# First stage of an MLP on seven half products, one more batch transposed through HBM, and a new plan of steps

## Chip, core and metric

The kernel runs on one core of a Trainium2 chip. The time is the device time of one execution in microseconds (us). Engines: PE (TensorE, matmuls; PEld is its weight load), DVE (VectorE), ACT (ScalarE), POOL (GpSimd, which also issues the loads' DMAs) and SP (whose queue issues stores and the DMAs of the round trips through HBM).

## What is computed

```python
# q, k, v: (8 batches, 8 heads, 576 rows, 64), float32
k_p = k.reshape(B, H, 72, 8, D).mean(axis=3)            # keys and values pooled by 8
v_p = v.reshape(B, H, 72, 8, D).mean(axis=3)
attn = softmax(q @ k_p.T / sqrt(D));  x = attn @ v_p     # x as (8, 576, 512)
h = relu(x.T @ w_tok1) @ w_tok2;      u = x + h.T        # w_tok1 (576, 256), w_tok2 (256, 576)
out = u + relu(u @ w_ch1) @ w_ch2                        # w_ch1 (512, 1536), w_ch2 (1536, 512)
```

## The kernel before

**Units.** The channel MLP (last line above) is done in nine units of 512 rows: unit n takes 512 of the 576 rows of batch n, and unit 8 takes the 64 rows left over of each of the eight batches. Everything else (pooling, scores, softmax, token MLP) is cut into named steps of batch n+1, n+2 and so on, and these are put between the matmuls of unit n.

**One unit.** First stage: 12 tiles of 128 hidden columns (`l1_tile`, L517), each 4 matmuls with 512 columns of `uT` (u transposed, 128 channels on partitions) as the moving side and a 128x128 block of `w_ch1` as weights, into one of four PSUM banks p1a to p1d; ACT writes relu of it to `GT` (L521). Second stage: the product with `w_ch2` in seven half-size products in place of eight (a Strassen-Winograd scheme), each 12 matmuls of 256 columns (`product`, L583). In order: x and y (both on plain `GT`), z, x again, w, z again, x again; unit 8 leaves w out and does its last two on x. DVE makes the sums of `GT` that they need: steps `=3`, `=1`, `=2`, `=4` (L545, L557), on 128x1536, into `area`; sums of `w_ch2` are made once (`w0` to `w3`). DVE also evacuates every product (L626), adding the residual u and earlier products. All of that is in program order on each engine.

**The plan.** `PLAN[n]` says which steps are recorded after which chunk of unit n. A chunk is what PE does between two yields: two matmuls of 512 columns in the first stage, four of 256 in the second. A normal unit has 45 chunks (24, then 3 for each of seven products). The plan fixes the order on each engine, and nothing else; each engine goes as fast as its waits allow. Steps named here: `b.K0 b.K1 b.V0 b.V1` pool k and v of batch b on POOL (L174 to L180); `b.kpT` transposes the pooled keys on PE (L222); `b.s0` to `s2` scores and exp; `b.av0` to `av4` the product with v; `b.at0 b.at1` and `b.u0` to `u4` the token MLP; `b.lk b.lq b.lv` loads. `g` is a gate: DVE sets a flag and POOL copies it (L712, L713), so that what POOL has next, a load or a pooling, starts no sooner than DVE gets there; the next gate's flag waits for the copy. `HEAD` is the same kind of list for what comes before unit 0; `d3` in it is three filler matmuls on zeros.

**From u to uT.** Two ways. Batches 1 and 2: steps `t0` to `t3`, each four 128x128 PE transposes into PSUM (L424) and one ACT copy (L425). Batches 3 to 7 (`BOUNCED`) and the left-over rows: u is spilled to HBM (`M0`, `M2`, for the left-over rows `M4`), read back by four DMAs (`M`, `MT`), all on SP's queue, and each of `T0` to `T3` (`T4`, `T5`) transposes it in 32x32 blocks on DVE (L458). The rows of u then lie in another order ("paired"), and an evacuation with such a residual is two DVE instructions of 256 columns in place of one of 512. Batch 0 has a way of its own through matmuls.

**Buffers.** Four PSUM banks are handed out by `take` and `give`, two more pairs are a pool of two (`ps_two`). `raw` holds two buffers each of loaded k, v and q.

The functions that the diff touches, as they were:

Of the kernel before, what the change touches and what calls it, by code (L numbers as in the profile page):

```python
# [8 lines left out]
FP32 = mybir.dt.float32  # L9
BF16 = mybir.dt.bfloat16  # L10
# [7 lines left out]
SYNC = mybir.EngineType.SP  # L18


HEAD = """LkA LkT LkB LvT Lq LvA LvB Lt1 Lk1 Lt2 Lc1b Lc1a Lq1 Lc1c Lv1 Lc1d p1 Lc2a Lc2b Lc2c d2 d2 d3 d1 d4 d4 c0 c1 prep q0 kp0 kp1 kt0 q1 d1 o0 kt1 kp2 e0 e1 q3 kt2 o1 q2 e3 vpool0 o3 e2 a00 vpool1 a02 o2 m01 d1 d1 m00 a04 X1 m03 a14 m02 X0 m04 p0 a10 a12 1.kpool m10 m14 m12 m13 m11 A1 A0 X2 X3 A2 A3"""
PLAN = [
# [9 lines left out]
]  # L32


# [1 line left out]
def kernel(  # L36
# [15 lines left out]
    B, H, S, D = q.shape  # L52
    P = 128
    POOL = 8
    BOUNCED = range(3, B)
    SP = S // POOL
    BP, BR = 64, S // 64
    NE = (BR + 1) // 2
# [60 lines left out]
                            in_=src[b, h0:h1].rearrange("h (j i) d -> j h (i d)", i=POOL)[j0:j1])  # L119

    def load_kv(b, src, key):
        t = loaded[b, key] = raw.tile([SP, H, POOL, D], BF16, name=key + "r")
        kv(t, src, b, 0, H, 0, BP)
        kv(t, src, b, 0, H, BP, SP)

# [3 lines left out]

    def first_kv(key, part):  # L130
        if (0, key) not in loaded:
            loaded[0, key] = raw.tile([SP, H, POOL, D], BF16, name=key + "r")
# [381 lines left out]
    def l1_tile(n, m, uT):  # L514
        ps = take([P, 512], FP32)
        for kk in range(4):
            nc.tensor.matmul(out=ps, lhsT=w_ch1[:, kk, m * P:(m + 1) * P], rhs=uT[kk],  # L517
                             start=(kk == 0), stop=(kk == 3))
            if kk == 1:
                yield  # L520
        nc.scalar.activation(out=GT[:, m, :], in_=ps, func=AF.Relu)  # L521
        give(ps)
        yield
# [39 lines left out]
    def weight_sum(k):  # L563
# [7 lines left out]
        else:  # L571
            sub(T[:, 3], w_ch2[:, sec, lo], T[:, 1])

    def unit_fast(n, u):
        last = n == B
        uT = [u["uT"][:, kk, :] for kk in range(4)]
        for m in range(NM):
            yield from l1_tile(n, m, uT)

        def product(ps, a, w, start, after, split=False, end=None):  # L580
            for i in range(2):
                for m in range(NH):
                    nc.tensor.matmul(out=ps[i] if split else ps[:, i], lhsT=chunk(u, i, a(m)), rhs=w(m),  # L583
                                     start=start and m == 0 and (i == 0 or split), stop=(m == NH - 1),
                                     skip_group_check=True)
                    if (i * NH + m) % 4 == 3 and (i, m) != (1, NH - 1):
                        yield
                if split:
                    after(i)
            if not split:  # L590
                after(slice(0, 2))
            if end is not None:
                give(end)
            yield

        def bank(split=False):
            if split:
                return [ps_two.tile([P, 2, 512], FP32, name="p2")[:, 0, 0:256] for _ in range(2)]
            return take([P, 2, 256], FP32)
# [17 lines left out]
        def plus(out, ps, other, then=None):  # L617
            def go(e):
                if type(e) is slice and len(other(e).shape) > 3:
                    go(0)  # L620
                    go(1)
                    return
                aps = [f(e) for f in (out, ps, other)]
                if len(aps[2].shape) == 4:
                    aps[:2] = [x.rearrange("p (k a f) -> p k a f", k=2, a=4) for x in aps[:2]]
                nc.vector.tensor_tensor(out=aps[0], in0=aps[1], in1=aps[2], op=ALU.add)  # L626
# [14 lines left out]
        x, y = bank(last), bank()  # L641
        s1 = keep("s1")
        yield from product(x, lambda m: GT[:, m, lo], lambda m: w_ch2[:, m, lo], True,
                           plus(part(s1), part(x), residual(0, 0)), last)
        yield from product(y, lambda m: GT[:, NH + m, lo], lambda m: w_ch2[:, NH + m, lo], True,
                           plus(cols_of(oa, 0), part(y), part(s1)), end=y)
# [68 lines left out]
    def unit(n, at):  # L715
        if n + 2 < B:
            batches[n + 2][0]()
        st = batches[n][2] if n < B else dict(uT=uT_tails, u=u_tails, paired=True)
        for i, _ in enumerate(unit_fast(n, st)):
            for s in at.get(i, "").split():  # L720
                if s[0] == "=":
                    g_sums(s[1:])
                elif s == "g":
                    gate()
                elif s[0] == "w":
                    weight_sum(int(s[1:]))
                else:
# [55 lines left out]
```

## Time and profile before

| | before |
|---|---|
| median of 3 runs | 266.96 us (266.85 to 267.04) |
| the profiled execution | 266.17 us, span 264.4 us |
| PE busy | 256.2 us, 97% of the span |
| DVE, ACT, POOL busy | 178.4, 119.6, 153.1 us |
| head, until the first matmul of L517 | 0 to 24.60 us |
| units 0 to 6 | 24.60 to 221.19 us |
| unit 7, unit 8 | 221.19 to 240.72, 240.72 to 264.4 us |
| mean granted PE clock | 0.999 |

The span runs from the first to the last instruction. A busy time counts the time in which an engine has an instruction under way; matmuls are pipelined, so the duration in a PE row (379 ns for 512 columns) is longer than the distance to the next one. "[0.92 <-POOL kp L178]" behind a row is idle time ahead of it and what ended it. The chain is followed back from the last instruction, at each step to what released it.

### The profile page before, as it was taken

Reading aid. Unit: us, or ns where it says so; the run is one execution under the profiler, and the core shown is the slowest. Engines: PE = TensorE matmul, PEld = TensorE weight load, DVE = VectorE, ACT = ScalarE, POOL = GpSimd, SP = SyncE. Lnnn points to the kernel's source line nnn. Section 1 sums busy time; section 2 is a strip of 40 time slices with the busy share of each in tenths; the row PEclk is TensorE's granted clock in tenths of the full one; section 3 lists DMA queues with packets and bytes.
Section 4 is the critical chain, followed back from the end, with each engine's and each line's share of the span. In section 5 each row is a group of like instructions: output and inputs, shape, how many; then the busy total and the mean of one; then the engine's idle time right before and its main releaser. Section 6 shows DMA issues by size and latency. Waiting matters only on the chain.

```text
span 264.4 us, 5328 instructions
## 1 busy us (share of the span) xinstructions
PE 256.2 (97%) x2121; PEld 160.3 (61%) x2121; DVE 178.4 (67%) x370; ACT 119.6 (45%) x195; POOL 153.1 (58%) x177
## 2 busy tenths in 40 slices
PE   8799999989999999999999999999999999999994
PEld 3685466744677545774487447744874486486483
DVE  3557569996787655895599678844795576184183
ACT  2355763149536456425641575165435412612700
POOL 8577326899999999988959982898200010100000
PEclk9999999999999999999999999999999999999999
DMA  6999999993088928699447940830513053404104
GB/s 141 193 195 206 205 207 208 205 216 80 4 129 141 166 82 171 149 202 266 91 132 107 232 144 17 158 94 4 159 38 122 30 170 80 121 0 102 59 0 159
DMA packets 31704, 34.29 MB, mean 130 GB/s; under 512 B 3136, under 2 KB 23744, under 8 KB 31680
## 3 DMA queue, kind: packets, MB, share of 16 engines
q0 software_dynamic: 17632, 17.64, 42.3%
q1 hardware_dynamic: 13632, 15.93, 20.2%
q10 hardware_dynamic: 416, 0.39, 0.5%
q8 instruction: 16, 0.26, 0.4%
q14 instruction: 8, 0.07, 0.1%
HBM read 38.99 MB, written 12.58 MB: 195 GB/s over the span
## 4 chain that ended last, share of the span: by engine, by line
PE 73%; DVE 12%; POOL 8%; issue 3%; DMA 2%; ACT 1%; POOLq 0%; ACTq 0%
PE p1c L517 10%; PE p1b L517 8%; PE p1a L517 7%; PE p1d L517 7%; PE p1d L583 6%; PE p1c L583 5%; PE p1b L583 4%; PE p1a L583 4%; POOL t L174 3%; PE p L297 3%; DVE x L384 3%; DVE area L545 3%; PE p L379 2%; DMA kr<-in_k_dram 2%; POOL t L175 2%
## 5 line engine op out<-in xcount | busy, mean ns | idle before, releaser
L517 PEld LDWEIGHTS <-w_ch 128*128 128x128 bf16 x432 | 39.5, 98 | 44.4 <-issue 2.7
L713 POOL COPY flag<-flag 1x1 f32<-1x1 f32 x47 | 15.3, 326 | 86.0 <-DVE flag L712 86.0
L583 PEld LDWEIGHTS <-area 128*128 128x128 bf16 x432 | 41.4, 98 | 7.8 <-issue 1.2
L306 ACT ACTIVATE ex<-p 72x768 bf16<-72x768 f32 x42 | 31.6, 803 | 17.1 <-PE p L297 17.1
L583 PEld LDWEIGHTS <-GT 128*128 128x128 bf16 x324 | 30.7, 98 | 7.9 <-issue 1.6
L175 POOL TENSOR_TENSOR t<-t 72x512 f32<-72x512 f32 x23 | 31.2, 1358 | 1.8
L517 PE MATMUL p1c<-uT,w_ch 128*128 128x512 bf16 x116 | 31.4, 379 | 0.0
L521 ACT ACTIVATE GT<-p1b 128x512 bf16<-128x512 f32 x27 | 16.1, 597 | 27.5 <-PE p1b L517 20.9
L521 ACT ACTIVATE GT<-p1c 128x512 bf16<-128x512 f32 x32 | 19.1, 598 | 15.5 <-PE p1c L517 11.7
L517 PE MATMUL p1b<-uT,w_ch 128*128 128x512 bf16 x96 | 26.0, 379 | 0.0
L174 POOL TENSOR_TENSOR t<-kr 72x1024 f32<-72x1024 bf16 x12 | 25.5, 2121 | 0.4
L174 POOL TENSOR_TENSOR t<-vr 72x1024 f32<-72x1024 bf16 x11 | 23.4, 2125 | 1.0 <-DMA vr<-in_v_dram 0.5
L517 PE MATMUL p1a<-uT,w_ch 128*128 128x512 bf16 x88 | 23.9, 379 | 0.0
L517 PE MATMUL p1d<-uT,w_ch 128*128 128x512 bf16 x84 | 22.2, 379 | 0.0
L521 ACT ACTIVATE GT<-p1a 128x512 bf16<-128x512 f32 x25 | 14.9, 597 | 15.4 <-PE p1a L517 14.8
L521 ACT ACTIVATE GT<-p1d 128x512 bf16<-128x512 f32 x24 | 14.4, 599 | 12.8 <-PE p1d L517 7.3
L384 DVE TENSOR_TENSOR x<-p,den 128x512 bf16<-128x512 f32 x28 | 19.3, 691 | 1.0
L545 DVE TENSOR_TENSOR area<-GT 128x1536 bf16<-128x1536 bf16 x9 | 11.3, 1257 | 11.9 <-ACT GT L521 6.7
L557 DVE TENSOR_TENSOR area<-GT 128x1536 bf16<-128x1536 bf16 x9 | 9.5, 1054 | 11.3 <-ACT GT L521 11.3
L379 PEld LDWEIGHTS <-ex 72*128 72x128 bf16 x280 | 12.9, 98 | 6.5 <-DVE x L384 1.4
L379 PE MATMUL p<-vp,ex 72*128 72x65 bf16 x280 | 14.4, 194 | 0.3 <-POOL vp L180 0.2
L118 POOL DMA_DIRECT2D kr<-in_k_dram x17 | 10.9, 646 | 5.6 <-PE p1b L222 1.9
(185 smaller groups left out, 464.2 us busy)
## 6 DMA issues: line engine op xcount, KB each, us to landing
out_dram<-o SPq DMA_DIRECT2D x32, 256.0 KB, 4.2
qb<-in_q_dram POOLq DMA_DIRECT2D x7, 576.0 KB, 9.4
kr<-in_k_dram POOLq DMA_DIRECT2D x7, 512.0 KB, 8.4
vr<-in_v_dram POOLq DMA_DIRECT2D x7, 512.0 KB, 14.0
w_ch<-in_moe_w_ch_dram POOLq DMA_DIRECT2D x5, 512.0 KB, 14.8
mem<-u SPq DMA_DIRECT2D x10, 256.0 KB, 2.2
v<-mem SPq DMA_DIRECT2D x20, 128.0 KB, 2.9
area<-in_q_dram SPq DMA_DIRECT2D x2, 288.0 KB, 3.0
```

The costliest lines, as they stand in the source:

```text
L118: nc.gpsimd.dma_start(out=t[j0:j1, h0:h1].rearrange("j h i d -> j h (i d)"), in_=src[b, h0:h1].rearrange("h (j i) d -> j h (i d)", i=POOL) ...
L174: eng.tensor_tensor(out=t4[:, 0:n], in0=t[:, hs, 0:4], in1=t[:, hs, 4:8], op=ALU.add)
L175: eng.tensor_tensor(out=t4[:, 0:n, 0:2], in0=t4[:, 0:n, 0:2], in1=t4[:, 0:n, 2:4], op=ALU.add)
L306: nc.scalar.activation(out=dst, in_=src, func=AF.Exp, scale=scale)
L379: nc.tensor.matmul(out=ps[:, h // 4, (h % 4) * (D + 1):(h % 4 + 1) * (D + 1)], lhsT=st["ex"][:, h * S + n0:h * S + n0 + P], rhs=st["vp"][: ...
L384: nc.vector.tensor_tensor(out=dst.rearrange("p (a h d) -> p a h d", a=2, d=D), in0=view[:, :, :, 0:D], in1=den[rows, :, :, None].broadcast ...
L517: nc.tensor.matmul(out=ps, lhsT=w_ch1[:, kk, m * P:(m + 1) * P], rhs=uT[kk], start=(kk == 0), stop=(kk == 3))
L521: nc.scalar.activation(out=GT[:, m, :], in_=ps, func=AF.Relu)
L545: nc.vector.tensor_tensor(out=out, in0=a, in1=b, op=ALU.subtract)
L557: nc.vector.tensor_tensor(out=S4[:, 0], in0=GT[:, f, hi], in1=GT[:, sec, hi], op=ALU.add)
L583: nc.tensor.matmul(out=ps[i] if split else ps[:, i], lhsT=chunk(u, i, a(m)), rhs=w(m), start=start and m == 0 and (i == 0 or split), stop= ...
L713: nc.gpsimd.tensor_copy(out=flag[:, 1:2], in_=flag[:, 0:1])
```

## The change

First stage of units 7 and 8 (`HALVED`). In place of 48 matmuls of 512 columns it runs three groups a, b, c. Each has seven products of four matmuls of 256 columns (`a1` to `a7` and so on). Four sums of blocks of `w_ch1` (`S1` to `S4`) are made once in unit 6, by steps `W0` to `W3` on DVE; four sums of blocks of `uT` (`T1` to `T4` in `row_sums`) are made for each of the two units by `D70` to `D73` and `D80` to `D83`. They lie in freed buffers of `raw`. Products build on each other in two PSUM banks per group; three times per group ACT copies a partial result to SBUF as fp32 (`kept`), three times DVE adds such a copy to a bank and writes `GT`, and POOL then takes the relu of that in place (`added`); once ACT writes relu straight from PSUM. The first two products of the second stage, x and y, are cut into three pieces each (`x0 x1 x2 y0 y1 y2`) and mixed with the groups' products. A unit of this kind has 42 chunks: the 27 of the string, and 3 for each of five products.

`BOUNCED` begins at batch 2: its `t0` to `t3` become `M0 M2 M` and `T0` to `T3`.

`HEAD` and all of `PLAN` are new. Of it, as far as it is spoken of later: HEAD has 18 filler matmuls where it had 19, and `1.vpool0` and `0.u1` stand at step 11 of unit 0 (before: 12 and 0). Unit 1: `2.u3 2.u2` at 26, `2.u0 2.u1` at 28, `2.M2` 33, `2.M0` 38, `2.M` 40, `2.T0 2.T1 2.T3` 42, `2.T2 3.av3` 43, `3.av0` 44; `3.V1` at 27 and `3.V0` at 30 (before: 36 and 39). Unit 5: `7.K0` at 17 and `7.kpT` at 19 (0 and 10). Unit 6: `W0` 8, `W1` 10, `W2` 18, `W3` 22, `D70` 41, `D72 D71` 43, `D73` 44. Unit 7: `7.T5` 14, `7.T4` 18, `=3` 21, `=1` 22, `=2` 24, `=4` 27, `D80` 32, `D81` 39, `D83` 40, `D82 g g g` 41. Unit 8: `g` 0, `=3` 19, `=1` 22, `=2` 24, `=4` 27.

```diff
-    BOUNCED = range(3, B)
+    BOUNCED = range(2, B)
+    HALVED = {B - 1: "b1 a1 a2 a5 b5 a6 b2 b6 a3 c1 b3 a7 b7 c5 c6 c2 c3 a4 c7 x0 b4 c4 x1 y0 y1 x2 y2",
+              B: "a1 a2 a5 b1 a6 b2 b5 a3 b6 a7 c1 b7 c2 c5 b3 c6 c3 a4 c7 b4 x0 c4 x1 x2 y0 y1 y2"}
...
+    def first_weight(k):
...
+        if k == 0:
+            nc.vector.tensor_tensor(out=S1, in0=w_ch1[:, c1, n2], in1=w_ch1[:, c2, n2], op=ALU.add)
+        elif k == 1:
+            sub(S2, S1, w_ch1[:, c1, n1])
...
+    def row_sums(n, k):
...
+        if k == 0:
+            sub(T1, uT[:, c1, lo], uT[:, c1, hi])
+        elif k == 1:
+            sub(T2, uT[:, c2, lo], T1)
...
+    def first_halved(n, uT, piece):
...
+            def mm(ps, a, col, b, start, stop):
+                for j in range(2):
+                    for c in range(2):
+                        o = col + (2 * g + j) * P
+                        nc.tensor.matmul(out=ps[:, j], lhsT=a[:, c, o:o + P], rhs=b[c], start=start and j == 0 and c == 0,
+                                         stop=stop and c == 1, skip_group_check=True)
...
+            def added(mr, cols, ps, other):
+                nc.vector.tensor_tensor(out=GT[:, mr, cols], in0=ps, in1=other, op=ALU.add)
+                nc.gpsimd.tensor_scalar(out=GT[:, mr, cols], in0=GT[:, mr, cols], scalar1=0.0, scalar2=None, op0=ALU.max)
+
+            def p1():
+                t["x"] = take([P, 2, 256], FP32)
+                mm(t["x"], w1, 0, half(u1, hi), True, False)
+                nc.scalar.copy(out=kept(0), in_=t["x"])
+
+            def p2():
+                y = take([P, 2, 256], FP32)
+                mm(y, w2, 0, half(u2, hi), True, True)
+                added(ms, hi, y, kept(0))
+                give(y)
+
+            def p5():
+                t["z"] = ps_two.tile([P, 2, 512], FP32, name="p2")[:, 0].rearrange("p (m n) -> p m n", m=2)
+                mm(t["z"], S1, 0, rows(T1), True, False)
+                nc.scalar.copy(out=kept(1), in_=t["z"])
+
+            def p6():
+                mm(t["x"], S2, 0, rows(T2), False, False)
+                nc.scalar.copy(out=kept(2), in_=t["x"])
+
+            def p3():
+                mm(t["z"], S4, 0, half(u2, lo), False, True)
+                added(ms, lo, t["z"], kept(2))
+
+            def p7():
+                mm(t["x"], S3, 0, rows(T3), False, False)
+                added(mt, lo, t["x"], kept(1))
+
+            def p4():
+                mm(t["x"], w2, DC // 2, rows(T4), False, True)
+                nc.scalar.activation(out=GT[:, mt, hi], in_=t["x"], func=AF.Relu)
+                give(t["x"])
...
     def unit_fast(n, u):
...
-        for m in range(NM):
-            yield from l1_tile(n, m, uT)
...
+        def piece(key, k):
+            split = last and key == "x"
+            t = two[key] = two.get(key) or bank(split)
+            o = NH * (key == "y")
+            for i, m in [(k, m) for m in range(4)] if k < 2 else [(i, m) for i in range(2) for m in (4, 5)]:
+                nc.tensor.matmul(out=t[i] if split else t[:, i], lhsT=chunk(u, i, GT[:, o + m, lo]), rhs=w_ch2[:, o + m, lo],
+                                 start=m == 0 and (i == 0 or split), stop=m == NH - 1, skip_group_check=True)
...
+        if n in HALVED:
+            yield from first_halved(n, uT, piece)
+            x = two["x"]
+        else:
+            for m in range(NM):
+                yield from l1_tile(n, m, uT)
...
```

More of the change, by code (lines that the diff above doesn't have):

```diff
@@ L121, in load_kv @@
     def load_kv(b, src, key):
-        t = loaded[b, key] = raw.tile([SP, H, POOL, D], BF16, name=key + "r")
+        t = loaded[b, key] = raw.tile([P, H, POOL, D], BF16, name=key + "r")[0:SP]
         kv(t, src, b, 0, H, 0, BP)
@@ L572, in weight_sum @@
             sub(T[:, 3], w_ch2[:, sec, lo], T[:, 1])
+    wide = {}
+    def first_weight(k):
+        if k == 0:
+            for key in "kv":
+                t = raw.tile([P, H, POOL, D], BF16, name=key + "r").rearrange("p h i d -> p (h i d)")
+                wide[key] = t[:, 0:4 * DC // 2].rearrange("p (s c n) -> p s c n", s=2, c=2)
+                wide[key, "u"] = t[:, 4 * DC // 2:4 * DC // 2 + 1024].rearrange("p (s c n) -> p s c n", s=2, c=2)
+        c1, c2 = slice(0, 2), slice(2, 4)
+        n1, n2 = slice(0, DC // 2), slice(DC // 2, DC)
+        S1, S2, S3, S4 = (wide[key][:, i] for key in "kv" for i in range(2))
+        if k == 0:
+            nc.vector.tensor_tensor(out=S1, in0=w_ch1[:, c1, n2], in1=w_ch1[:, c2, n2], op=ALU.add)
+        elif k == 1:
+            sub(S2, S1, w_ch1[:, c1, n1])
+        elif k == 2:
+            sub(S3, w_ch1[:, c1, n1], w_ch1[:, c1, n2])
+        else:
+            sub(S4, w_ch1[:, c2, n1], S2)
@@ new lines, in row_sums, with group @@
+    def row_sums(n, k):
+        uT = batches[n][2]["uT"] if n < B else uT_tails
+        T1, T2, T3, T4 = (wide[key, "u"][:, i] for key in "kv" for i in range(2))
+        c1, c2 = slice(0, 2), slice(2, 4)
+        if k == 0:
+            sub(T1, uT[:, c1, lo], uT[:, c1, hi])
+        elif k == 1:
+            sub(T2, uT[:, c2, lo], T1)
+        elif k == 2:
+            sub(T3, uT[:, c2, lo], uT[:, c1, lo])
+        else:
+            sub(T4, uT[:, c2, hi], T2)
+    def first_halved(n, uT, piece):
+        S1, S2, S3, S4 = (wide[key][:, i] for key in "kv" for i in range(2))
+        T1, T2, T3, T4 = (wide[key, "u"][:, i] for key in "kv" for i in range(2))
+        spare = [raw.tile([P, H, POOL, D], BF16, name=key + "r").rearrange("p h i d -> p (h i d)").bitcast(FP32)
+                 .rearrange("p (s m n) -> p s m n", s=4, m=2) for key in "kv"] if n == min(HALVED) else wide["spare"]
+        wide["spare"] = spare
+        def group(g):
+            ms, mt = slice(2 * g, 2 * g + 2), slice(NH + 2 * g, NH + 2 * g + 2)
+            t = {}
+            def mm(ps, a, col, b, start, stop):
[4 more added lines that the diff above has]
+                                         stop=stop and c == 1, skip_group_check=True)
+            u1, u2 = ([uT[c] for c in cs] for cs in ((0, 1), (2, 3)))
+            half = lambda b, cols: [x[:, cols] for x in b]
+            rows = lambda T: [T[:, c] for c in range(2)]
+            w1, w2 = w_ch1[:, 0:2], w_ch1[:, 2:4]
+            kept = lambda i: spare[i // 2][:, 2 * (g % 2) + i % 2]
+            def added(mr, cols, ps, other):
[27 more added lines that the diff above has]
+                give(t["x"])
+            return {1: p1, 2: p2, 3: p3, 4: p4, 5: p5, 6: p6, 7: p7}
+        G = [group(g) for g in range(3)]
+        for s in HALVED[n].split():
+            if s[0] in "abc":
+                G["abc".index(s[0])][int(s[1])]()
+            else:
+                piece(s[0], int(s[1]))
+            yield
@@ L640, in unit_fast @@
         oa, ob = (outp.tile([P, 2, DM], FP32, name="o") for _ in range(2))
-        x, y = bank(last), bank()
         s1 = keep("s1")
[L643 to L646, printed above, removed]
+        evacuate = {"x": lambda e: plus(part(s1), part(two["x"]), residual(0, 0))(e),
+                    "y": lambda e: plus(cols_of(oa, 0), part(two["y"]), part(s1))(e)}
+        two = {}
+        def piece(key, k):
[5 more added lines that the diff above has]
+                                 start=m == 0 and (i == 0 or split), stop=m == NH - 1, skip_group_check=True)
+                if split and m == NH - 1:
+                    evacuate[key](i)
+            if k == 2 and not split:
+                evacuate[key](slice(0, 2))
+            if k == 2 and key == "y":
+                give(t)
+        if n in HALVED:
+            yield from first_halved(n, uT, piece)
+            x = two["x"]
+        else:
+            for m in range(NM):
+                yield from l1_tile(n, m, uT)
+            x, y = bank(last), bank()
+            yield from product(x, lambda m: GT[:, m, lo], lambda m: w_ch2[:, m, lo], True,
+                               plus(part(s1), part(x), residual(0, 0)), last)
+            yield from product(y, lambda m: GT[:, NH + m, lo], lambda m: w_ch2[:, NH + m, lo], True,
+                               plus(cols_of(oa, 0), part(y), part(s1)), end=y)
         z = bank()
```

8 lines of the change are left out of this document (6 added, 2 removed), and 18 rows, old and new, of the table PLAN.

## The prediction

> **What bounds the kernel now.** I read the page's busy shares and chain first, then busy time by stretch, then the timelines of TensorE (PE), VectorE (DVE) and GpSimd (POOL) around the places that the change touches.
>
> ```profile
> PE 256.2 (97%) x2121; PEld 160.3 (61%) x2121; DVE 178.4 (67%) x370; ACT 119.6 (45%) x195; POOL 153.1 (58%) x177
> PE 73%; DVE 12%; POOL 8%; issue 3%; DMA 2%; ACT 1%; POOLq 0%; ACTq 0%
> ```
>
> PE is busy nearly always and holds most of the chain that ended last. Busy time by stretch (columns: stretch, length, then busy time of PE, PEld, DVE, ACT, POOL, each with its instructions; clock, DMA share, GB/s):
>
> ```profile
> 24.60:57.58 32.98, 32.06 (x276) 20.11 (x275) 26.00 (x46) 15.91 (x26) 18.51 (x22) 1.00 1.23 206
> 196.60:221.19 24.59, 24.59 (x175) 15.21 (x172) 16.81 (x38) 8.26 (x14) 1.35 (x4) 1.00 0.32 97
> 221.19:240.72 19.53, 19.53 (x134) 12.91 (x132) 9.94 (x25) 7.16 (x12) 1.91 (x7) 1.00 0.26 68
> ```
>
> These are units 0, 6 and 7. From the middle on PE has no gap at full clock, so time goes only where a matmul goes. Unit 0 alone loses about 0.9. PE's timeline gives the pitch of each kind, from one group's start to the next:
>
> ```profile
> 57.50 0.24 PE L222 MATMUL p1c<-ident,kp 72*128 72x72 bf16 x2 [0.92 <-POOL kp L178]
> 85.44 0.39 PE L424 MATMUL p1c<-ident,u 128*128 128x128 bf16 x4
> 85.66 0.60 PE L583 MATMUL p1a<-area,area 128*128 128x256 bf16 x4
> 229.83 1.03 PE L517 MATMUL p1c<-uT,w_ch 128*128 128x512 bf16 x4
> 230.69 1.03 PE L517 MATMUL p1d<-uT,w_ch 128*128 128x512 bf16 x4
> 231.56 1.47 PE L583 MATMUL p1b<-w_ch,GT 128*128 128x256 bf16 x12
> 232.87 1.47 PE L583 MATMUL p1a<-w_ch,GT 128*128 128x256 bf16 x12
> 256.78 1.47 PE L583 MATMUL p1d<-w_ch,area 128*128 128x256 bf16 x12 [0.29 <-DVE s L626]
> ```
>
> A 512-column matmul takes 864/4 = 216.1 ns, a 256-column one with its own weight load 1310/12 = 109.2 ns, four transposes 0.22 us. Unit 8 runs from 240.72 to 259.42 + 1.31 = 260.73, 20.01 us, of which 0.46 is the stall ahead of 256.78 (the group before began at 255.01 and needs 1.31). The rows that price the new work on POOL and DVE:
>
> ```profile
> 3.53 0.29 POOL masks.py:199 TENSOR_SCALAR_AFFINE_SELECT ident<-ident 128x128 bf16<-128x128 bf16 x1
> 20.49 1.28 POOL L159 COPY w_tok<-area 128x576 bf16<-128x576 bf16 x1
> 240.39 0.17 POOL L713 COPY flag<-flag 1x1 f32<-1x1 f32 x1 [4.28 <-DVE flag L712]
> 230.82 0.86 POOL L713 COPY flag<-flag 1x1 f32<-1x1 f32 x1 [0.17 <-DVE flag L712]
> 230.69 0.95 DVE L545 TENSOR_TENSOR area<-GT 128x1536 bf16<-128x1536 bf16 x1 [0.28 <-ACT GT L521]
> 51.44 1.62 DVE L545 TENSOR_TENSOR area<-w_ch 128x1536 bf16<-128x1536 bf16 x1
> ```
>
> **The change part by part.** (1) *First stage of units 7 and 8.* Out: 12 tiles x 4 = 48 matmuls of 512 columns, 48 x 0.2161 = 10.37 us. In: 3 groups x 7 products x 4 = 84 of 256 columns, 84 x 0.1092 = 9.17. Each unit saves 1.20 on PE if nothing waits.
>
> (2) *Batch 2 by HBM.* Out: 16 PE transposes, 4 x 0.22 = 0.88 us on PE, and 4 ACT copies. In: two spills and four reads on SP's queue, and four DVE block transposes of about 0.34 pitch. The last u of unit 1 comes at step 28, the first block transpose at 42: 14 x 0.437 plus three score steps of 0.56 is 7.8 us. Batch 7's round trip, from its last spill issue near 211.0 to its reads' issue at 213.1 to 214.9 plus a landing of 2.9, is 6.8, so the data is there; SP has no stores between. But the four transposes stand behind DVE's z evacuation of step 41 and end some 2.2 us after it, while PE gets to unit 2 after 1.31 + 0.52 (two av): I charge 0.4. Against that, 3.V0 moves from step 39 to 30, which takes away the wait of 0.20 to 0.3 at 86.69 that came from POOL's pooling of v. Part: -0.88 + 0.4 - 0.3 = -0.8.
>
> (3) *Head and unit 0.* One filler matmul less: -0.2. The stall of 0.92 at 57.50 ends POOL's chain of pooling 2.k, which starts behind DVE's sums. With 1.vpool0 a step earlier, one u step added ahead of the avs, and the same sums, DVE gets through some 0.5 earlier; between nothing and 0.6 I take 0.2. Part: -0.4.
>
> (4) *Sums.* W0 to W3 in unit 6 are four DVE sums of 128x1536 at 0.95: DVE is busy 16.8 of 24.6 there, so 3.8 fit; POOL has 1.35 of work. D70 to D83 are 128x512 bf16 sums; no row has one, the block transpose of the same bytes is 0.42 and the 1536 row 0.95; I take 0.35 of pitch. They stand between the evacuations at the unit's end, which is why the next unit's sums begin late.
>
> (5) *Evacuation of the first stage*, the part that decides. Before: 12 ACT relus of 0.60. After, per unit: 12 ACT copies or relus (same), 9 DVE sums from PSUM (row L626, 128x512: 0.68, pitch 0.63), and behind each a POOL relu of 128x512 bf16 in place, duration r, in program order. No row shows it. From below: the in-place one-input bf16 op on 128 partitions (293 ns for 128 columns) and the one-element copy (174) give 0.94 ns per column, r = 0.65. From above: the L159 copy, (1278-174)/576 = 1.92 ns per column, r = 1.16; its source has a stride of 9 elements, and the same copy on ACT takes 1253 where a dense 512 takes 586, so dense must be well under. I take 0.72, by the first row, the nearest in type, density and partitions, with the memset's slope (237 to 100 ns over 127 columns, 1.08).
>
> The Trainium skill, GPSIMD Engine Reference, section 3.1, puts a tight loop near 1.8 cycles per element, 769 ns for 512, and section 4.1 advises against elementwise work there; by its figure r would be an estimated 0.77 and the sum 0.2 to 0.3 higher. No run here shows it.
>
> *Unit 7*, times from the end E of unit 6's matmuls. DVE does D70, D72, D71 and the two last evacuations to +2.35, D73 to +2.7; the first sum ends at 3.4. POOL then runs 9 relus from 3.5: the k-th ends at 3.5 + k r. Product x2 (step 25, due 10.92) needs the 8th: 9.3. y2 (due 11.36) needs the 9th: 10.0. The =3 sum follows the 8th, =1 waits for ACT's relu of c4 (10.45) and ends at 11.4; z is due 11.79. =2 ends 12.3, x is evacuated by 13.0, due 13.1. No wait: -1.20.
>
> *Unit 8.* The four gates at its start (three in step 41, one in step 0) hold DVE by 0.37 each: last evacuations to 1.43, D82 to 1.8, gates to 2.95, first sum to 3.65, POOL from 3.75. x0 (due 8.74) needs the 7th relu: 3.75 + 7 x 0.72 = 8.8, a stall of 0.13. =3, =1, the x evacuation, =2, the y evacuation, =4 and s5 then follow on DVE from 9.6 to 15.2 (0.87, 0.87 after c4's relu, 0.67, 0.87, 0.65, 0.87, 0.67), and the second z product, due 14.55, waits for s5: 0.65. Net: -1.20 + 0.13 + 0.65 - 0.46 = -0.88.
>
> The shared-port cost: the flag copy above takes 0.17 alone and 0.86 beside the DVE sum of two SBUF inputs, and that kind of sum 1.62 beside POOL's pooling. The new DVE sums have one input in PSUM; only =3 overlaps the last relus. I add 0.3 for that and for small waits that new plans bring.
>
> The Trainium skill, GPSIMD Engine Reference, section 1, says that the interface is shared with VectorE instructions with two SBUF inputs; by that rule the PSUM sums leave the relus alone, and the flag rows agree.
>
> **Sum.** -0.8 - 0.4 - 1.20 - 0.88 + 0.3 = -3.0 against the profiled execution, 266.17 us (span 264.4 and 1.8 around it): 263.2. The median of runs, 266.96, lies 0.8 above that execution: 264.0; leaning a little to r above 0.72, **264.2**.
>
> **Rivals.** *A. POOL becomes the bound (slower).* It decides from r of about 0.93. At r = 1.0 unit 7 waits 1.24 ahead of y2, then 0.46 for =1 and 0.25 for the x evacuation: +0.75 net; unit 8 waits 2.06 ahead of x0 and 1.0 later, 0.46 gone: +1.40. With -0.9 from the rest, 266.96 + 1.25 = 268.2. At r = 1.16 the waits are 3.26 and 4.3, less 0.46: some 270.8. For it: the L159 row, and POOL's two-input 72x512 row (L175, 1.36). Against: stride, second input.
>
> *B. The waits eat the gain.* Relus near 0.88 (unit 8 loses 1.25 more at x0, unit 7 0.3) or a port conflict of 0.7 a piece on two or three of them, or a round trip of batch 2 or a pooling that comes 1 us late in units 1 to 6 (7.K0 at step 17 has 1.7 us before 7.kpT): 265.3 to 266.9. For: 45 and 42 steps, all re-placed, with DVE as the late engine at each unit's end. Against: by the walk, units 1 to 6 keep 1.4 to 3.5 us between a pooling's end and its kpT.
>
> *C. More than forecast.* r of 0.65, unit 0's stall down by 0.5, none of the 0.3: 263.2.
>
> **How the numbers follow.** Forecast 0.56, C 0.14, B 0.14, A 0.16. The likeliest case's own range is 263.5 to 265.2. The range 262.9 to 267.4 takes in C, B and the near part of A and leaves out most of A (0.13) and a little below. A measurement can tell 0.2%, 0.53 us, from no change. Faster (under 266.43): forecast, C and 0.06 of B, 0.76; same: the rest of B and 0.01 of A, 0.09; slower: 0.15 of A.
>
> **What would show it.** Right: the new matmul line at a pitch near 109 ns; POOL's relu row at 0.6 to 0.85; unit 7 some 18.3 long, unit 8 some 19.1; no L424. Wrong: PE waits on POOL's GT row ahead of the x and y products, or a relu row of 0.93 or more; a wait at the start of unit 2 of over 0.5; a new idle PE ahead of a kpT or a score.

## The result, and the profile after

The changed kernel takes 277.9 us (median of 4, 277.23 to 278.3) against 266.9 for the kernel before: a ratio of 1.042, 95% interval 1.038 to 1.046. It is slower by 11 us where 2.8 less was forecast. The profiled execution took 278.3 us with a span of 276.5.

The page's busy shares, then its chain by engine, then PE and its granted clock in 40 slices of the span:

```profile
PE 257.3 (93%) x2154; PEld 167.9 (61%) x2176; DVE 199.7 (72%) x407; ACT 116.2 (42%) x191; POOL 181.0 (65%) x194
PE 39%; POOL 6%; DVE 4%; issue 1%; POOLq 0%; DVEq 0%
PE   8999899989999999999999999999999997699294
PEclk9999999999999999999999999999999999799779
```

The last fifth has changed its nature: PE idles there and its clock drops with it. Busy time by stretch, units 0, 6, 7 and 8 (columns as in the prediction):

```profile
24.65:58.17 33.52, 31.96 (x272) 19.96 (x275) 26.46 (x48) 15.75 (x26) 18.74 (x25) 1.00 1.23 205
196.98:221.58 24.60, 24.49 (x174) 15.23 (x172) 19.96 (x46) 8.26 (x14) 3.69 (x9) 1.00 0.37 104
221.58:246.88 25.30, 20.86 (x170) 16.78 (x168) 18.01 (x35) 6.57 (x12) 13.43 (x10) 0.93 0.18 46
246.88:272.76 25.88, 20.93 (x170) 17.44 (x167) 16.49 (x34) 6.87 (x12) 14.74 (x15) 0.87 0.18 53
```

Up to unit 7 the two kernels are level (221.58 against 221.19). Unit 7 then takes 25.30 us for 19.53 and unit 8 25.88 for 20.01: 5.8 to 5.9 each, nearly all of the 12.1 us by which the span grew. In both, POOL has 13 us or more of work where it had 1.9 and 0.5. Its group on the page, and the two runs of relus in POOL's timeline:

```profile
L635 POOL TENSOR_SCALAR GT<-GT 128x512 bf16<-128x512 bf16 x18 | 26.2, 1482 | 3.1 <-DVE GT L634 3.1
224.80 13.12 POOL L635 TENSOR_SCALAR GT<-GT 128x512 bf16<-128x512 bf16 x9 [2.53 <-DVE GT L634]
250.72 13.09 POOL L635 TENSOR_SCALAR GT<-GT 128x512 bf16<-128x512 bf16 x9 [0.54 <-DVE GT L634]
```

Behind the bar stand busy us and mean ns of one; in a timeline, start and length. A relu takes 1.48 us, not the 0.72 of the prediction, and nine stand back to back: 13.1 us of POOL beside 9.2 us of matmuls. PE's timeline shows who pays. L624 is a product of the first stage, L754 a piece of x or y, L686 the rest of the second stage:

```profile
221.58 0.60 PE L624 MATMUL p1d<-uT,w_ch 128*128 128x256 bf16 x4
222.01 0.60 PE L624 MATMUL p1a<-uT,w_ch 128*128 128x256 bf16 x4
...
233.63 0.83 PE L754 MATMUL p1a<-w_ch,GT 128*128 128x256 bf16 x6 [0.98 <-POOL GT L635]
236.53 0.61 PE L754 MATMUL p1c<-w_ch,GT 128*128 128x256 bf16 x4 [2.07 <-POOL GT L635]
237.98 0.61 PE L754 MATMUL p1a<-w_ch,GT 128*128 128x256 bf16 x4 [0.84 <-POOL GT L635]
238.79 2.74 PE L686 MATMUL p1d<-area,area 128*128 128x256 bf16 x12 [0.20 <-DVE area L559]
241.33 1.79 PE L686 MATMUL p1c<-area,area 128*128 128x256 bf16 x12
242.95 1.47 PE L686 MATMUL p1b<-area,GT 128*128 128x256 bf16 x12
...
260.97 0.61 PE L754 MATMUL p<-w_ch,GT 128*128 128x256 bf16 x2 [4.95 <-POOL GT L635]
```

The products themselves run as forecast, 0.437 us for four. Each wait ends on POOL's relu: 4.95 us in one piece in unit 8, and 0.35, 0.98, 2.07 and 0.84 in unit 7. A second loss stands behind them. The 12 matmuls at 238.79 take 2.54 us, the next 12 take 1.62, and only the third lot has its 1.31 again: behind the waits PE runs at half speed, 0.213 us a matmul for 0.109, for 3.2 us in unit 7 and 4.9 in unit 8. The granted clock agrees: 0.50 from 238.8 to 241.3 us, 0.51 from 261 to 266.

### The profile page after: what moved, and what is told of

Its sections match the earlier page's. It is cut to its first block, busy times and chain, and to the rows that moved or that the text cites. A ratio compares the mean times of both kernels' runs of the same rounds, so it can differ in the third digit from the quotient of the medians.

```text
span 276.5 us, 5489 instructions
## 1 busy us (share of the span) xinstructions
PE 257.3 (93%) x2154; PEld 167.9 (61%) x2176; DVE 199.7 (72%) x407; ACT 116.2 (42%) x191; POOL 181.0 (65%) x194
## 4 chain that ended last, share of the span: by engine, by line
PE 39%; POOL 6%; DVE 4%; issue 1%; POOLq 0%; DVEq 0%
POOL GT L635 6%; PE p1c L686 4%; PE p1d L686 4%; PE p1a L686 4%; PE p1b L519 4%; PE p1b L686 3%; PE p1a L519 3%; PE p1d L519 3%; PE p1c L519 2%; PE p L686 1%; DVE o L729 1%; PE p L381 1%; PE p L299 1%; PE p L754 1%; PE p1c L754 1%
## 5 line engine op out<-in xcount | busy, mean ns | idle before, releaser
L840 POOL COPY flag<-flag 1x1 f32<-1x1 f32 x46 | 16.7, 364 | 58.5 <-DVE flag L839 58.3
L519 PEld LDWEIGHTS <-w_ch 128*128 128x128 bf16 x336 | 30.5, 98 | 34.3 <-issue 1.9
L686 PEld LDWEIGHTS <-area 128*128 128x128 bf16 x432 | 41.5, 100 | 8.3 <-issue 1.0
L686 PEld LDWEIGHTS <-GT 128*128 128x128 bf16 x276 | 26.3, 98 | 7.3 <-issue 2.0
L635 POOL TENSOR_SCALAR GT<-GT 128x512 bf16<-128x512 bf16 x18 | 26.2, 1482 | 3.1 <-DVE GT L634 3.1
L547 DVE TENSOR_TENSOR area<-GT 128x1536 bf16<-128x1536 bf16 x9 | 13.0, 1449 | 14.8 <-POOL GT L635 11.6
L519 PE MATMUL p1a<-uT,w_ch 128*128 128x512 bf16 x76 | 21.3, 379 | 0.3 <-issue 0.2
L519 PE MATMUL p1c<-uT,w_ch 128*128 128x512 bf16 x70 | 18.5, 379 | 0.3 <-issue 0.3
L523 ACT ACTIVATE GT<-p1a 128x512 bf16<-128x512 f32 x20 | 12.0, 598 | 11.4 <-PE p1a L519 6.7
L523 ACT ACTIVATE GT<-p1d 128x512 bf16<-128x512 f32 x21 | 12.6, 599 | 8.1 <-PE p1d L519 7.6
L686 PE MATMUL p1c<-area,area 128*128 128x256 bf16 x108 | 13.7, 276 | 0.0
```

Of the source, the lines that this page charges most:

```text
L547: nc.vector.tensor_tensor(out=out, in0=a, in1=b, op=ALU.subtract)
L635: nc.gpsimd.tensor_scalar(out=GT[:, mr, cols], in0=GT[:, mr, cols], scalar1=0.0, scalar2=None, op0=ALU.max)
L840: nc.gpsimd.tensor_copy(out=flag[:, 1:2], in_=flag[:, 0:1])
```

## Experiments: is it the relus?

The theory: POOL's nine relus bound the first stage of units 7 and 8, and the clock adds to that. The rivals: the new plans of units 0 to 6 cost time; the halved scheme is held by DVE whoever does the relu. Three kernels take the change apart, and a fourth asks why the relu costs 1.48.

**Relus on DVE.**

```diff
-                nc.gpsimd.tensor_scalar(out=GT[:, mr, cols], in0=GT[:, mr, cols], scalar1=0.0, scalar2=None, op0=ALU.max)
+                nc.vector.tensor_scalar(out=GT[:, mr, cols], in0=GT[:, mr, cols], scalar1=0.0, scalar2=None, op0=ALU.max)
```

> The changed kernel with the nine relus of each halved unit on DVE (same place in the order, in place on GT) in place of POOL. Theory (nine POOL relus of 1.48 us, 13.1 us in a row, bound the first stage of units 7 and 8): the waits on POOL's GT row go, and a DVE relu of 128x512 bf16 costs at most the 0.35 pitch of the two-input sum of the same size, so DVE needs 9 x (0.63 + 0.35) = 8.8 us from about 2.4 us (unit 7) and 3.1 us (unit 8) into the unit, some 0.5 to 1.5 us late for x and y: units 7 and 8 at 19.0 to 20.5 us each in place of 25.3 and 25.9, PE at full clock throughout, time 265.5 to 268. Rival 1 (the new plans of units 0 to 6, not the relus, cost several us): stays above 270. Rival 2 (the halved first stage is held by DVE's chain at its end whoever does the relu): units 7 and 8 stay above 22 us each.

Measured: 267.66 us, 1.004 (1.0015 to 1.0064) of before, 10 us under the changed kernel by one word. Unit 7 took 20.2 us, unit 8 21.0, at full clock. A DVE relu is 0.29 us long, but a sum and the relu that waits for it come every 0.93 us, where sums alone come every 0.6 to 0.63:

```profile
223.84 0.68 DVE L634 TENSOR_TENSOR GT<-p1c,kr 128x512 bf16<-128x512 f32 x1
224.56 0.29 DVE L635 TENSOR_SCALAR GT<-GT 128x512 bf16<-128x512 bf16 x1
224.77 0.68 DVE L634 TENSOR_TENSOR GT<-p,vr 128x512 bf16<-128x512 f32 x1
```

So DVE is late in its turn (the longest waits of PE for it are 0.82 us in unit 7 and 1.13 in unit 8). Both rivals fall as causes of the 11 us: the plans are the same here, and the units are well under 22.

**Relus left out.**

```diff
-                nc.gpsimd.tensor_scalar(out=GT[:, mr, cols], in0=GT[:, mr, cols], scalar1=0.0, scalar2=None, op0=ALU.max)
+                pass
```

> The changed kernel without the relu of nine of the twelve parts of GT (the part left out is max(.,0) after the DVE sums; the three relus of ACT stay). It prices the relus. Theory: POOL has nothing in the first stage of units 7 and 8; DVE needs 9 x 0.63 = 5.7 us there; unit 7 comes to about 18.3 us and unit 8 to about 19.1 (the prediction's own figures), time 277.9 - 7.0 - 6.8 = 264.1, with units 0 to 6 unchanged at 221.6. Rival (halving has another bound, DVE's late sums =3, =1, =2, =4 or the gates): 0.5 to 2 us more in unit 8, 264.6 to 266.

Measured: 263.55 us. The stretches of units 7 and 8, and the only wait that PE's timeline lists in them:

```profile
220.34:238.87 18.53, 18.53 (x170) 16.44 (x168) 17.39 (x35) 6.58 (x12) 0.30 (x1) 1.00 0.25 62
238.87:258.03 19.16, 18.61 (x170) 16.30 (x167) 15.93 (x34) 6.87 (x12) 1.04 (x6) 1.00 0.25 72
254.08 0.38 PE L686 MATMUL p1a<-w_ch,area 128*128 128x256 bf16 x2 [0.55 <-DVE s L729]
```

18.53 us against 19.53 before: with the relus gone unit 7 saves 1.00 of the 1.20 us that seven half products should save, and the rest goes in gaps of about 0.1 us. Unit 8, at 19.16 for 20.01, still has the late s5 (DVE's evacuation of z, which the second z product waits for). The relus cost 25.30 - 18.53 = 6.8 us in unit 7 and 25.88 - 19.16 = 6.7 in unit 8.

**The new plans alone.** Unit 6 without `W0` to `W3` and `D70` to `D73`, the plans of units 7 and 8 as in the kernel before (but `7.MT`, which stands in unit 6 now).

```diff
...
-    HALVED = {B - 1: "b1 a1 a2 a5 b5 a6 b2 b6 a3 c1 b3 a7 b7 c5 c6 c2 c3 a4 c7 x0 b4 c4 x1 y0 y1 x2 y2",
-              B: "a1 a2 a5 b1 a6 b2 b5 a3 b6 a7 c1 b7 c2 c5 b3 c6 c3 a4 c7 b4 x0 c4 x1 x2 y0 y1 y2"}
+    HALVED = {}
```

> The changed kernel with the head and the plans of units 0 to 6 as changed (batch 2 by way of HBM), but units 7 and 8 as before: first stage in 12 tiles, no sums W0 to W3 and D70 to D83, steps of units 7 and 8 as before. Theory from the trace of after: the part is worth about nothing, unit 6 ends within 0.4 us of where it ended before (221.2 to 221.6), time 266.8 to 267.4. The prediction's sum for these parts (-0.8 and -0.4): 265.7. Rival (the extra DMA and block transposes of batch 2 cost later): over 267.5.

Measured: 265.66 us (12 runs), 0.9964 (0.9939 to 0.9989) of before, whose median beside it was 266.4: a gain of 0.0036 x 266.4 = 0.96 us (0.3 to 1.6 by the interval), near the prediction's 1.2. The profiled executions show only 0.15 of it (unit 6 ends at 221.04 for 221.19), so the theory's reading of the two traces, that the part is worth nothing, was too rough. A limit of such readings shows here: ten kernels whose units 0 to 6 hold the same instructions ended unit 6 between 220.34 and 221.79 us, with the first matmul of unit 0 between 23.77 and 24.92. Below, units 7 and 8 are compared by their own lengths.

**Forms of a POOL operation**, on spare tiles behind the last evacuation of the kernel with the new plans alone.

```diff
+        for _ in range(3):
+            relu(nc.gpsimd, g, g)
+        for _ in range(3):
+            relu(nc.gpsimd, t[:, 0:512], t[:, 0:512])
+        for _ in range(3):
+            relu(nc.gpsimd, t[:, 0:512], t[:, 512:1024])
...
```

> The kernel of the run before this one with a row of probes behind its last evacuation, on spare tiles, when nothing else runs: on POOL max(.,0) on bf16, three of each: 128 x (2 x 256, stride 512) in place, 512 dense in place, 512 dense into another tile, 256 dense, 128 dense, 512 of fp32, then a copy of 512 bf16, a two-input sum of 512 bf16, a memset of 512 bf16; then the first form on DVE and on ACT; then POOL's 512 dense beside DVE sums of two SBUF inputs, and beside DVE sums of PSUM and SBUF. Only the rows count, not the time. H1 (a TENSOR_SCALAR on POOL costs about 2.55 ns per column whatever the view): 1.48, 1.48, 1.48, 0.83, 0.5, and the copy of 512 well under 1.48 or the same. H2 (the cut view or the update in place costs): dense or out of place near 0.72. H3 (port conflict with DVE): all near 0.72 alone and 1.48 only beside DVE. DVE's relu is expected at 0.2 to 0.42 us, ACT's at 0.55 to 0.6.

POOL's groups by form, when nothing else runs (the x9 are the cut view in place, dense in place, and dense into another tile):

```profile
L894 POOL TENSOR_SCALAR kr<-kr 128x512 bf16<-128x512 bf16 x9 | 13.4, 1485 | 6.7 <-DVE kr L890 6.1
L894 POOL TENSOR_SCALAR kr<-kr 128x512 f32<-128x512 f32 x3 | 4.4, 1483 | 0.2
L911 POOL TENSOR_TENSOR kr<-kr 128x512 bf16<-128x512 bf16 x3 | 3.4, 1148 | 0.2
L894 POOL TENSOR_SCALAR kr<-kr 128x256 bf16<-128x256 bf16 x3 | 2.5, 844 | 0.2
L909 POOL COPY kr<-kr 128x512 bf16<-128x512 bf16 x3 | 1.8, 610 | 0.1
L894 POOL TENSOR_SCALAR kr<-kr 128x128 bf16<-128x128 bf16 x3 | 1.6, 524 | 0.2
```

H1 holds. The view, the update in place and the type change nothing; 128, 256 and 512 columns give 0.52, 0.84 and 1.48, that is 0.20 us and 2.5 ns a column. A sum of two inputs is cheaper than this one-input operation, and a copy costs less than half. Why is not shown. H3 falls: the 1.48 needs no DVE. Three relus beside DVE, first with sums of two SBUF inputs beside the last two of them, then with sums of PSUM and SBUF:

```profile
297.90 6.01 POOL L894 TENSOR_SCALAR vr<-vr 128x512 bf16<-128x512 bf16 x3 [1.61 <-DVE vr L918]
304.65 4.50 POOL L894 TENSOR_SCALAR vr<-vr 128x512 bf16<-128x512 bf16 x3 [0.74 <-DVE vr L924]
```

Beside DVE sums of PSUM and SBUF a relu stays at 1.48; beside DVE sums of two SBUF inputs the two took 2.29 and 2.19. The Trainium skill, GPSIMD Engine Reference, section 1, says that the interface is shared with VectorE instructions that have two inputs in SBUF; these rows agree. Section 3.1 of that page of the Trainium skill gives 769 ns for 512 elements as the best loop; this TENSOR_SCALAR takes 1.9 times that.

## Experiments: from the relu's length to the time

**Which row was wrong.** The prediction had its 0.94 ns a column from an affine select of 128 columns. The same place, with other operations:

> The kernel with the new plans alone, and behind its last evacuation another row of probes on POOL, when nothing else runs, two of each, bf16 in place unless said: the affine select of the identity on 128 and on 512 columns; a copy of 128 and of 512 into other columns; a copy of 512 whose source has a stride of 64 elements; a TENSOR_SCALAR mult by 0 on 128 and 512, an add of 0 on 512, a max with 0 on 512. Only the rows count, not the time. H1 (the slope belongs to the kind of instruction: the affine select, whose 293 ns for 128 columns gave the prediction its 0.94 ns per column, is cheap, every TENSOR_SCALAR is not): affine select 0.29 and about 0.65, mult and add 1.48 like max. H2 (max alone is slow): mult and add near the 0.61 of the copy. H3 (the affine select has a hidden fixed cost and the same slope as max): over 1 us for 512.

```profile
L888 POOL TENSOR_SCALAR kr<-kr 128x512 bf16<-128x512 bf16 x6 | 8.9, 1488 | 0.5
L901 POOL COPY kr<-kr 128x512 bf16<-128x512 bf16 x2 | 2.2, 1077 | 0.1
L899 POOL COPY kr<-kr 128x512 bf16<-128x512 bf16 x2 | 1.2, 613 | 0.1
L891 POOL TENSOR_SCALAR_AFFINE_SELECT kr<-kr 128x512 bf16<-128x512 bf16 x2 | 1.2, 612 | 0.1
L891 POOL TENSOR_SCALAR_AFFINE_SELECT kr<-kr 128x128 bf16<-128x128 bf16 x2 | 0.6, 292 | 3.4 <-DVE kr L885 3.3
```

H1 again: an affine select of 512 columns takes 0.61, close to the 0.65 that the prediction worked out from it, and mult, add and max (the x6) all take 1.49. The row was read rightly and belonged to another kind of instruction. A copy with a strided source takes 1.08, so the copy of L159 as well told of its stride and not of a TENSOR_SCALAR.

**Shorter relus.** On 256 of the 512 columns, then on 384 (`0:192` in place of `0:128`); the other columns are left without a relu:

```diff
-                nc.gpsimd.tensor_scalar(out=GT[:, mr, cols], in0=GT[:, mr, cols], scalar1=0.0, scalar2=None, op0=ALU.max)
+                nc.gpsimd.tensor_scalar(out=GT[:, mr, cols][:, :, 0:128], in0=GT[:, mr, cols][:, :, 0:128], scalar1=0.0, scalar2=None, op0=ALU.max)
```

> The changed kernel with each POOL relu on half of its columns, 128 x (2 x 128) in place of 128 x (2 x 256) (the relu of the other half is left out). It sets r to 0.84, the row that the probes gave for 256 columns, and tests the prediction's way from r to the time (no waits to speak of below 0.93, slower above). By the walk: unit 8 waits about 0.9 ahead of x0 and 0.5 to 0.7 later, unit 7 about 0 to 0.3, time 264.5 to 265.5 where r of 0 gave 263.55. Rival (POOL between DVE and PE costs by its latency and not by its length alone): over 266.5.

> The changed kernel with each POOL relu on 384 of its 512 columns, 128 x (2 x 192) (the relu of the other quarter is left out). By the probes' slope (2.5 ns a column and 0.20 us) r is 1.16, the upper end that the prediction had taken from the copy of L159, for which its rival A gave 270.8 us (waits of 3.26 us in unit 7 and 4.3 us in unit 8, less 0.46). Theory (the walk from r to the time was right and only r was not): 270 to 271.5; unit 7 at about 21.5 and unit 8 at about 22.9. Rival (the time grows by more than the waits, since PE's clock falls behind a wait of 2 to 3 us): 272 or more, with matmuls at over 150 ns behind the wait ahead of x0.

| columns | relu | unit 7 | unit 8 | median |
|---|---|---|---|---|
| 0 (left out) | 0 | 18.53 | 19.16 | 263.55 |
| 256 | 0.85 | 18.93 | 20.08 | 265.93 |
| 384 | 1.16 | 22.62 | 22.91 | 271.17 |
| 512 | 1.48 | 25.30 | 25.88 | 277.9 |

From 0 to 0.85 us the two units grow by 1.3 us, from 0.85 to 1.16 by 6.5: the deciding point lies between, where the prediction put it (0.93). The median with 256 columns is 0.4 us over its expected range; in the profiled execution the units' own growth is the 1.3, and unit 6 ends 1.2 later than with no relu. Rival A of the prediction gave 270.8 for 1.16, and 271.17 came (270.14 to 272.57). With 384 columns unit 7 is 1.1 us over the expectation, and that is the clock, as the rival of the expectation said, though the time stayed under that rival's 272. PE's timeline of that run:

```profile
232.95 0.61 PE L754 MATMUL p1c<-w_ch,GT 128*128 128x256 bf16 x4 [1.11 <-POOL GT L635]
234.08 0.61 PE L754 MATMUL p1a<-w_ch,GT 128*128 128x256 bf16 x4 [0.52 <-POOL GT L635]
235.11 2.74 PE L686 MATMUL p1d<-area,area 128*128 128x256 bf16 x12 [0.41 <-DVE area L559]
```

Unit 8 came at the expected 22.9, but not by the expected way: its one listed wait is 2.69 us where 4.3 were priced, and the matmuls behind it ran at half speed (granted clock 0.55 from 255.2 to 259.0) in place of the later waits. So the agreement with 270.8 is in part luck.

**The waits filled**, to price the clock: matmuls that nobody reads, in PE's waits and nearly as long.

```diff
+        def fill(count):
+            ps = take([P, 512], FP32)
+            for _ in range(count):
+                nc.tensor.matmul(out=ps, lhsT=ident, rhs=w_ch1[:, 0, 0:512], start=True, stop=True)
+            give(ps)
+
+        fills = {("x", 0, 0, 2): 20} if last else {("y", 0, 0, 2): 4, ("x", 2, 0, 4): 9, ("y", 2, 0, 4): 3}
```

> The changed kernel (relus on POOL) with matmuls of 512 columns that nobody reads put into PE's waits for POOL's relus: 4 + 9 + 3 in unit 7 (ahead of the third matmul of y0 and the first of x2 and y2), 20 in unit 8 (ahead of the third matmul of x0), 0.216 us each at full clock, a little less than the waits are long. They add work and take away idle time alone. Theory (after a wait of some us PE runs its next matmuls at about half clock, and that costs unit 7 about 1.4 us and unit 8 about 1.8): the waits end when they did, the 12 matmuls of z in unit 7 take 1.31 us in place of 2.54 and the 20 behind x0 in unit 8 take their 109 ns each, time 274 to 275.5. Rival (those matmuls were slow for another reason, or the filler delays the work behind it): 277.5 or more.

Measured: 276.16 us, 1.034 (1.030 to 1.038) of before. Unit 7 fell to 24.09 (1.2 less) and unit 8 to 25.40 (0.5 less); the granted clock of both stretches is 1.00. In unit 7 the waits end where they did (x2 goes on 14.9 us into the unit in both), so the filler holds nothing up there. PE behind the waits:

```profile
238.24 1.49 PE L686 MATMUL p1b<-area,area 128*128 128x256 bf16 x12 [0.20 <-DVE area L559]
262.91 1.49 PE L686 MATMUL p1b<-area,area 128*128 128x256 bf16 x12 [0.21 <-DVE area L559]
266.58 1.47 PE L686 MATMUL p1b<-w_ch,area 128*128 128x256 bf16 x12 [0.65 <-DVE s L729]
```

So the half speed is real and goes when PE is kept busy, but it costs 1.7 us and not the expected 3.2; the time lies between the theory's range and the rival's. In unit 8 DVE's sums, which begin late for the same relus, hold z and s5 (0.21 and 0.65) once PE is fast. The Trainium skill, TensorE: Matmul & The Clock Gate, Part 1, gives half clock after an idle window of about 3.4 us and full clock after about 3.4 us of work. The stretches of half speed (3.2 to 4.9 us) roughly fit that; the drop with 384 columns in unit 7 came without any single wait over 1.11 us, in a stretch of 3.5 us of which 2.0 were idle.

## Experiments: a version that pays

**Relus on two engines.** POOL keeps the four whose readers come last, DVE takes five; then also without the gates at the end of unit 7 and in unit 8, behind which POOL has no load or pooling left.

```diff
-            def added(mr, cols, ps, other):
+            def added(mr, cols, ps, other, eng=nc.vector):
...
-                nc.gpsimd.tensor_scalar(out=GT[:, mr, cols], in0=GT[:, mr, cols], scalar1=0.0, scalar2=None, op0=ALU.max)
+                eng.tensor_scalar(out=GT[:, mr, cols], in0=GT[:, mr, cols], scalar1=0.0, scalar2=None, op0=ALU.max)
...
-                added(ms, hi, y, kept(0))
+                added(ms, hi, y, kept(0), nc.gpsimd)
...
-                added(mt, lo, t["x"], kept(1))
+                added(mt, lo, t["x"], kept(1), nc.vector if g else nc.gpsimd)
```

> The changed kernel with the nine relus of a halved unit shared out: POOL keeps four (the three of product 2, and that of a7, whose readers come last), DVE takes the other five, each behind its sum. Theory: POOL needs 4 x 1.48 = 5.9 us and is through by about 9.4 us into the unit, ahead of =3; DVE needs 9 x 0.65 + 5 x 0.27 = 7.2 us from 2.4 us on (3.1 in unit 8), through at 9.6 to 10.3, so that neither is late by more than a few tenths: unit 7 at 18.5 to 19.2, unit 8 at 19.2 to 20.2, time 263.5 to 265.5. Rival (two engines in turn cost semaphore latency and port conflicts as much as the DVE-only version did): 267 or more.

```diff
-    {14: "7.T5", 18: "7.T4", 21: "=3", 22: "=1", 24: "=2", 27: "=4", 32: "D80", 39: "D81", 40: "D83", 41: "D82 g g g", 45: "g g"},
-    {0: "g", 19: "=3", 21: "g", 22: "=1", 24: "=2", 25: "g", 27: "=4"},
+    {14: "7.T5", 18: "7.T4", 21: "=3", 22: "=1", 24: "=2", 27: "=4", 32: "D80", 39: "D81", 40: "D83", 41: "D82"},
+    {19: "=3", 22: "=1", 24: "=2", 27: "=4"},
```

> The run before this one, and also without the gates recorded at the end of unit 7 and in unit 8, behind which no load or pooling is left. Theory: DVE's first sums of unit 8 start about 1.2 us earlier, the sum =3 ends ahead of the relu of c4, and the wait of 0.55 us for s5 ahead of the second z product goes: unit 8 at 18.4 to 18.8, time 0.4 to 1 us under the run before this one, 263.0 to 264.5, faster than both kernels. Rival (the gates lie beside other work): no difference to the run before this one.

Measured: 266.13 us (units 19.70 and 19.97), and 265.58 (19.70 and 19.52), 0.9956 (0.9936 to 0.9977) of before. The gates cost unit 8 0.45 us, but the two are 0.6 and 1.1 us over their expected ranges: PE waits 0.58 and 0.34 in unit 7 for copies and banks that DVE's sums free late, and s5 is still 0.53 late without the gates.

**Three engines**, ACT with two of the relus, no gates, and in unit 8 y's evacuation recorded behind z's.

```diff
+                if eng is nc.scalar:
+                    eng.activation(out=GT[:, mr, cols], in_=GT[:, mr, cols], func=AF.Relu)
...
+        if last:
+            evacuate["y"](slice(0, 2))
         s2 = keep("s1")
```

> The changed kernel without the idle gates of unit 8, with the relus of a halved unit shared out among three engines (POOL a2, b2, c2 and a7; ACT a3 and b7; DVE b3, c3 and c7), and in unit 8 with the evacuation of y recorded behind that of z. Theory (DVE's 0.93 us for a sum and its relu is what is left over: 0.5 to 0.9 us of gaps in each unit; and s5 comes 0.7 us late in unit 8 because y's evacuation of 0.69 us is ahead of it on DVE): unit 7 at 18.5 to 19.0, unit 8 at 18.4 to 18.9, against 19.70 and 19.52 in the run with two engines and no gates (265.58 us): 263.6 to 264.6, faster than both kernels. Rival (ACT, standing behind a DVE sum, hands its copies on late, and PE waits for those): no better than 265.3.

Measured: 267.25 us, 1.002 (0.9997 to 1.0043); the rival won. ACT, standing behind a DVE sum, hands on its copies late:

```profile
230.50 0.60 PE L624 MATMUL p<-uT,vr 128*128 128x256 bf16 x4 [1.56 <-ACT kr L654]
247.81 0.60 PE L624 MATMUL p1d<-vr 128*128 128x256 bf16 x4 [0.68 <-ACT vr L658]
```

The wait for s5 is no longer listed, though, with y's evacuation behind z's: by the distance of the groups 0.2 us is left of it.

**Two engines, relus late.** As the version without gates, with that move of y, and with DVE's relus of a3 and c3, in unit 7 of b3 too, recorded behind a later sum; the other DVE relus still stand behind their own.

```diff
...
+                else:
+                    pending.append(GT[:, mr, cols])
+                while flush and pending:
+                    part_of_GT = pending.pop(0)
+                    nc.vector.tensor_scalar(out=part_of_GT, in0=part_of_GT, scalar1=0.0, scalar2=None, op0=ALU.max)
...
```

> The kernel with the relus on two engines and no idle gates (POOL a2, b2, c2, a7; DVE a3, b3, b7, c3, c7), but DVE's relus recorded behind a later sum (a3 and b3 behind b7's sum, c3's behind c7's), so that the sums, which free banks and copies, come first; and in unit 8 y's evacuation is recorded behind z's. Theory: the gaps of 0.74 and 0.51 us in unit 7 and 0.45 in unit 8 (sums late on DVE) and 0.70 in unit 8 (s5 late) mostly go: unit 7 at 18.5 to 18.9, unit 8 at 18.4 to 18.9, 263.3 to 264.5, some 1.9 us under the version that it comes from (265.58) and some 1% under the kernel before. Rival (the gaps have another cause): 265 or more.

Measured: 264.7 us (7 runs), 0.9946 (0.9924 to 0.9967) of before: faster than both kernels, a little over the expected range. Units 7 and 8:

```profile
220.82:240.34 19.52, 19.10 (x170) 16.34 (x168) 18.59 (x40) 6.68 (x12) 6.38 (x5) 1.00 0.23 59
240.34:259.13 18.79, 18.70 (x170) 16.29 (x167) 16.94 (x33) 6.87 (x12) 5.96 (x4) 1.00 0.25 73
```

Unit 8 is where it was expected, unit 7 saves nothing against the kernel before (DVE is busy 18.6 of 19.5 us there, with the block transposes of the left-over rows). The gain over the new plans alone (0.9964) is not settled by the ratios, whose intervals overlap; by the lengths of units 7 and 8 it is 39.54 - 38.31 = 1.2 us.

## Why the prediction was wrong

The step that failed is the size of one term: r, the POOL relu, taken as 0.72 us between bounds of 0.65 and 1.16; it measured 1.48, above both. With it, and with the clock behind its waits, the sum's -1.20 for unit 7 became +5.8, and its -0.88 for unit 8 became +5.9. The lower bound was the slope of an affine select, the upper one that of a strided copy, and neither row was a TENSOR_SCALAR. Likeness in type, density and partitions was taken for likeness in cost. "Dense must be well under" the strided copy holds for the copy (0.61 against 1.08) and not for the relu. The figure of the Trainium skill, GPSIMD Engine Reference, section 3.1, 0.77 by the prediction's estimate, would not have saved it. The Trainium skill's rule against elementwise work on this engine, GPSIMD Engine Reference, section 4.1, names the better place here, 267.66 us with the relus on DVE for 277.9, but that is still no gain over the kernel before.

The forecast's own path, no wait in unit 7 and 0.13 us at x0 in unit 8, fell with r; the mechanism that took its place was named as a rival and priced. Rival A, POOL as the bound with PE waiting ahead of the x and y pieces, is what happened, and its deciding point lies inside the measured bracket. Its price at r = 1.16 held to 0.4 us, in part by luck (shorter waits, and a loss of clock that the price had not). Its way from r to the time, taken on to r = 1.48, gives an estimate of 275.7: 5.46 + 0.71 - 1.20 in unit 7, 5.37 + 1.0 - 0.46 - 1.20 in unit 8, -0.9 for the rest. The version with its waits filled, which keeps the clock, took 276.16. The chance given to rival A was too small, since the range of r stopped where rows of other instructions stopped.

Missing altogether was the clock: behind PE's waits the next 3 to 5 us of matmuls ran at half speed, 1.7 us of the 11 by the version with filled waits.

Point by point, for the rest:
- First stage: right. 109 ns a matmul; without relus 18.53 and 19.16 us against some 18.3 and 19.1.
- Batch 2 and unit 0: the sum of -1.2 measured -0.96 by the medians, but its terms came out otherwise, so that the sum is in part luck. In the profiled execution with the new plans alone unit 1 saves 1.04, units 2 to 6 lose 0.83, and unit 0 ends no earlier (57.64 for 57.58). The stall at the end of unit 0 went from 0.92 to 0.65 (0.2 forecast) and the wait at 86.69 is gone; the 0.4 charged at the start of unit 2 did not appear. In its place come waits of 0.23 for a pooled k, 0.55 for a pooled v and 0.41 for x in units 2 to 4, more than the 0.3 kept for new plans.
- Sums W and D: right. Unit 6 takes 24.60 for 24.59.
- Port: right for the PSUM sums. The =3 beside the last relus took 1.36 for 0.95, as foreseen; it waited for them anyway.
- Unit 8: the wait of 0.65 for s5 was forecast and is 0.55 with the relus out; the gates' delay was walked rightly and costs 0.45.

## What to carry to other kernels

A duration may be carried along a row's slope only within one kind of instruction on one engine; where an engine's next work is a kind that no row shows, its range is open upwards, and the forecast needs the length at which it becomes the bound before it needs a best guess. Where a step adds a relu behind a sum, record it behind the sums that free buffers, and not on an engine whose next work others wait for: ACT had slack here, and its copies came late. Waits of PE that add up, here 2.0 us within 3.5, can cost more than their length, since the matmuls behind them may run at half speed; behind a single wait of 1.56 us (three engines, unit 7) the granted clock stayed at 1.00.

## What the runs showed of the hardware that was not expected

- POOL's TENSOR_SCALAR on 128 partitions: 0.20 us and 2.5 ns a column, the same for bf16 and fp32, for max, mult and add, in place or not. Its copy and affine select of 512 columns take 0.61, its sum of two inputs 1.15. DVE does the same relu in 0.29, ACT in 0.63.
- PE at half speed, 0.213 us a matmul of 256 columns for 0.109, after 3.5 us with waits of 1.11, 0.52 and 0.41 us, as well as after one wait of 4.95.
- A DVE sum and a relu that waits for it come every 0.93 us; a group of sums alone every 0.6, and three relus in a row took 0.80.
